# Moving every weight and work buffer of a convolution-plus-feed-forward kernel to multiples of 2 KB

## The chip, the cores and the metric

The kernel runs on one core of a Trainium2 chip. The metric is the device time of one execution in microseconds (us); lower is better. Engines are named as in the profile: PE (TensorE matmuls), PEld (TensorE weight loads), DVE (VectorE), ACT (ScalarE), POOL (GpSimd), SP (SyncE). On-chip memory has 128 partitions, and a tile occupies the same range of bytes in each of them; "at byte n" means n bytes from the start of a partition.

## What is computed

The input x is [8, 4096, 192] in float32. Eight heads of 24 channels each get their own causal filter of seven taps, whose weights are a softmax over the taps. The result, seen as 32,768 tokens of 192 channels, goes through a feed-forward layer with a rational activation:

```python
w = softmax(weight)                        # [8 heads, 7 taps]
x[b, s, head] = sum_k w[head, k] * x_padded[b, s + k, head]
h = x @ w_in                               # 192 -> 2048
P = a0 + a1*h + a2*h**2 + a3*h**3
Q = 1 + |b0|*|h| + |b1|*h**2
out = (P / (Q + 1e-6)) @ w_out             # 2048 -> 192
```

Everything is float32 and must stay near float32 accuracy.

## The kernel before, in words

The 32,768 tokens are worked in 64 chunks of 512. For each chunk, PE computes the filter as many small banded matmuls (L299) from the input tile xs (two buffers of 6,912 bytes, one for even and one for odd chunks) and the band tile wb_t. ACT and DVE bring the result to memory as a high part xh and a low part xl, 2,048 bytes each, in the reduced float32 form float32r that PE reads.

The first matrix product, here gemm1 (L334), is cut into 8 units for each chunk, each a [128, 2 x 512] tile hp: ten matmuls for a unit, five for each half, which use the weights wh_t (high part) and wl_t (low part, 16,384 bytes each) as stationary operand and xh or xl as moving operand of 512 columns. With 64 chunks that makes 512 units and 5,120 matmuls. For each unit, ACT, POOL and DVE compute the rational function: ACT copies hp to hs (L379) and makes A = |.| (L399) and B = the square (L402); POOL makes t from hs (L385, L392) and issues a DMA that adds B to A in memory (L405); ACT takes the logarithm (L408) and the exponential, y (L411); DVE does four instructions of 128 x 1024 (L396, L415, L420, L424), of which the last writes g, the activated unit.

The second product, gemm2 (L351), uses slices of g (512 bytes) as stationary operand and slices of wo_t (192 columns, 768 bytes) as moving operand, in plain float32: 4,096 matmuls in the code, each of which stands as two records in the profile. ACT copies each result to ob, and SP stores it.

The order of all this is written out by hand: the strings START, PLAN and END give the order of steps for the first chunks, for each chunk in the middle and for the last ones, and each engine follows it. The tile framework puts in the semaphores. Before the loop, the weights are loaded, rounded and split into high and low parts.

Memory: a pool is a region, and the pools lie one behind another in the order in which they are opened: const, xpool (xh, xl), work (t, A, B, four buffers each), hpool (hs, three), gpool (g, eleven), opool (ob, two), apool. Within const the tiles lie in the order of the `const.tile` calls, each rounded up to 32 bytes. Bytes 0 to 16,511 are taken by a scratch area of 16,384 bytes and four constants. These are the places of the large tiles in the kernel before:

| tile | byte | past a multiple of 2,048 | past a multiple of 256 |
|---|---|---|---|
| wb_t | 16,512 | 128 | 128 |
| xs0, xs1 | 18,400 and 25,312 | 2,016 and 736 | 224 and 224 |
| wh_t, wl_t, wo_t | 32,224, 48,608, 64,992 | 1,504 | 224 |
| one_t, neg_t, cf, sq, mx, sm | 77,280 to 78,431 | | |
| xh, xl; t, A, B; hs; g; first ob | from 78,432 | 608 | 96 |

Of the kernel before, what the change touches and what calls it, by code (L numbers as in the profile page):

```python
# [10 lines left out]
F32 = mybir.dt.float32  # L11
F32R = mybir.dt.float32r
# [12 lines left out]
P = 128  # L25
# [9 lines left out]
NG = 6  # L35
# [77 lines left out]
def kernel(  # L113
# [14 lines left out]
    const = ctx.enter_context(tc.tile_pool(name="const", bufs=1))  # L128
# [13 lines left out]
    mk_t = const.tile([P, BW], F32, name="mk_t")  # L142
    wr_t = const.tile([P, NG, KT], F32, name="wr_t")
    ab_t = const.tile([P, 6], F32, name="ab_t")
    nc.scalar.dma_start(out=wr_t, in_=wrep)
    nc.scalar.dma_start(out=ab_t, in_=ab)
    nc.scalar.dma_start(out=wb_t, in_=wband)
# [1 line left out]
    W = 2 * CH  # L149
    XF = 32 * NBLK * NG  # L150
    xs_buf = [const.tile([P, XF], F32, name=f"xs{i}") for i in range(2)]

    def clear_x(t):
        nc.gpsimd.memset(t[0:BLK, 3 * XF // 4:], 0.0)
        nc.gpsimd.memset(t[BLK:, 0:3 * XF // 4], 0.0)
# [31 lines left out]
    nc.scalar.preload_act_table_set("natural_log_exp_and_others")  # L187


    one_t = const.tile([P, P], F32, name="one_t")  # L190
    neg_t = const.tile([P, P], F32R, name="neg_t")
    nc.gpsimd.memset(one_t, 1.0)
    nc.gpsimd.affine_select(out=one_t, in_=one_t, pattern=[[1, P]], compare_op=ALU.is_equal, fill=0.0,
                            base=0, channel_multiplier=-1)
# [10 lines left out]
    load_x(1)  # L205


    cf = const.tile([P, 6], F32, name="cf")
    sq = const.tile([P, 2], F32, name="sq")
    a0, a1, a2, a3 = (cf[:, i:i + 1] for i in range(4))  # L210
    be0, be1 = cf[:, 4:5], cf[:, 5:6]
    sq1, rq = sq[:, 0:1], sq[:, 1:2]
    mx = const.tile([P, NG], F32, name="mx")
    sm = const.tile([P, NG], F32, name="sm")
    nc.vector.tensor_reduce(out=mx, in_=wr_t, axis=AX.X, op=ALU.max)
    nc.vector.tensor_tensor(out=wr_t, in0=wr_t, in1=mx[:, :, None].broadcast_to([P, NG, KT]), op=ALU.subtract)
    nc.scalar.activation(out=wr_t, in_=wr_t, func=AF.Exp)
# [313 lines left out]
```

## Time and profile before

| | |
|---|---|
| median of 3 runs | 2,733.33 us (2,733.18 to 2,734.33) |
| time of the profiled execution | 2,734.59 us |
| its span, first to last instruction | 2,732.9 us |
| mean granted clock of TensorE | 0.997 of full speed |
| busy: PE / DVE / ACT / POOL | 2,696.7 / 2,588.5 / 2,563.2 / 2,318.2 us |

The busy time of an engine is the time in which at least one of its instructions runs; matmuls overlap at their ends in the record, so the pace of PE is read from the distance between starts, not from the length of one record. A wait is named by the instruction that waited and the one that released it.

### The profile page before, as it was taken

To read this page: it belongs to the slowest core of one execution; us is meant where nothing else is said; L and a number is where in the kernel's file an instruction comes from. 1 tells how busy PE (TensorE), PEld (TensorE's weight loads), DVE (VectorE), ACT (ScalarE), POOL (GpSimd) and SP (SyncE) were. 2 spreads that over 40 slices of the span, in tenths; PEclk is the share of its full clock that TensorE was granted. 3 is DMA by queue.
4 is the path that set the end of the run, shared out by engine and by line. 5 is a ranking of instruction groups with operands and counts; after the bars stand their busy time and mean duration, and the time that the engine had idled before them with its cause. 6 is when DMAs were issued, how large, how long until landed. Compare 5 with 4: busy or idle time off the path is not lost.

```text
span 2732.9 us, 51350 instructions
## 1 busy us (share of the span) xinstructions
PE 2696.7 (99%) x20248; PEld 2418.7 (89%) x20248; DVE 2588.5 (95%) x2285; ACT 2563.2 (94%) x2927; POOL 2318.2 (85%) x1575
## 2 busy tenths in 40 slices
PE   6999999999999999999999999999999999999999
PEld 4898899898989998998998889989989998899898
DVE  7999999999999999999999999999999999999997
ACT  7999999999999999999999999999999999999996
POOL 9888888888888888888888888888888888888885
PEclk9999999999999999999999999999999999999999
DMA  7565566656665656656666656565666565666654
GB/s 188 108 124 120 120 126 120 124 117 122 123 121 118 126 119 123 123 119 124 121 121 123 120 117 128 117 126 120 119 123 125 116 125 119 120 125 121 124 104 92
DMA packets 122786, 332.79 MB, mean 122 GB/s; under 512 B 12848, under 2 KB 51888, under 8 KB 122544
## 3 DMA queue, kind: packets, MB, share of 16 engines
q0 software_dynamic: 73728, 268.47, 51.9%
q1 hardware_dynamic: 48384, 60.83, 7.9%
q8 instruction: 159, 2.61, 0.4%
q14 instruction: 83, 0.68, 0.1%
q10 hardware_dynamic: 432, 0.20, 0.0%
HBM read 35.85 MB, written 25.17 MB: 22 GB/s over the span
## 4 chain that ended last, share of the span: by engine, by line
PE 95%; ACT 2%; POOL 1%; issue 1%; DVE 1%; DMA 0%; ACTq 0%; POOLq 0%; DVEq 0%
PE op L351 48%; PE hp L334 43%; PE cps L299 4%; POOL t L392 0%; PE cps L351 0%; ACT hs L379 0%; ACT A L399 0%; ACT y L411 0%; ACT B L408 0%; DMA A<-B 0%; ACT B L402 0%; POOL t L385 0%; DMA wb_t<-in_wband 0%; DVE t L396 0%; ACT op L252 0%
## 5 line engine op out<-in xcount | busy, mean ns | idle before, releaser
L351 PE MATMUL op<-wo_t,g 128*128 128x192 f32 x8128 | 1412.3, 327 | 0.9 <-DVE wo_t L266 0.7
L351 PEld LDWEIGHTS op<-wo_t,g 128*128 128x128 f32 x8128 | 1342.7, 190 | 45.0 <-POOL t L392 1.4
L392 POOL TENSOR_TENSOR t<-t,hs 128x1024 f32<-128x1024 f32 x512 | 1267.7, 2476 | 31.8
L385 POOL TENSOR_SCALAR t<-hs,cf 128x1024 f32<-128x1024 f32 x512 | 646.8, 1263 | 299.9 <-ACT hs L379 294.5
L334 PE MATMUL hp<-xh,wh_t 128*128 128x512 f32 x2048 | 878.2, 429 | 10.1 <-DVE t L396 9.7
L415 DVE SCALAR_TENSOR_TENSOR g<-t,cf,y 128x1024 f32<-128x1024 f32 x512 | 655.2, 1280 | 91.5 <-ACT y L411 74.9
L396 DVE SCALAR_TENSOR_TENSOR t<-t,cf,hp 128x1024 f32<-128x1024 f32 x512 | 651.9, 1273 | 6.0 <-POOL t L392 4.0
L379 ACT COPY hs<-hp 128x1024 f32<-128x1024 f32 x512 | 525.3, 1026 | 133.2 <-PE hp L334 128.7
L424 DVE SCALAR_TENSOR_TENSOR g<-y,g 128x1024 f32<-128x1024 f32 x512 | 626.9, 1224 | 17.5
L334 PE MATMUL hp<-xh,wl_t 128*128 128x512 f32 x2048 | 643.3, 395 | 0.0
L420 DVE SCALAR_TENSOR_TENSOR y<-A,y 128x1024 f32<-128x1024 f32 x512 | 625.7, 1222 | 0.0
L408 ACT ACTIVATE B<-A 128x1024 f32<-128x1024 f32 x512 | 551.2, 1077 | 2.4 <-DMA A<-B 2.4
L411 ACT ACTIVATE y<-B 128x1024 f32<-128x1024 f32 x512 | 536.5, 1048 | 3.2 <-DVE g L424 2.3
L405 POOL DMA_DIRECT2D A<-B x512 | 481.1, 940 | 65.6 <-ACT A L399 42.0
L399 ACT ACTIVATE A<-hp 128x1024 f32<-128x1024 f32 x512 | 532.7, 1040 | 0.5 <-PE hp L334 0.5
L402 ACT ACTIVATE B<-hp 128x1024 f32<-128x1024 f32 x512 | 529.3, 1034 | 1.5
L334 PEld LDWEIGHTS hp<-xh,wh_t 128*128 128x128 f32 x2048 | 387.3, 189 | 89.7 <-DVE t L396 12.6
L334 PEld LDWEIGHTS hp<-xh,wl_t 128*128 128x128 f32 x2048 | 385.8, 188 | 88.7
L334 PE MATMUL hp<-xl,wh_t 128*128 128x512 f32 x1024 | 404.7, 395 | 0.0
L334 PEld LDWEIGHTS hp<-xl,wh_t 128*128 128x128 f32 x1024 | 195.9, 191 | 22.6
L299 PEld LDWEIGHTS cps<-wb_t,xs 128*32 128x32 f32 x6876 | 121.3, 150 | 53.9 <-issue 49.5
L299 PE MATMUL cps<-wb_t,xs 128*32 128x58 f32 x6876 | 137.6, 228 | 16.3 <-DVE wb_t L224 13.2
(56 smaller groups left out, 381.6 us busy)
## 6 DMA issues: line engine op xcount, KB each, us to landing
A<-B POOLq DMA_DIRECT2D x512, 512.0 KB, 4.8
out<-ob SPq DMA_DIRECT2D x128, 192.0 KB, 2.0
xs<-in_xa SPq DMA_DIRECT2D x64, 324.0 KB, 4.0
xs<-in_xb SPq DMA_DIRECT2D x64, 108.0 KB, 3.8
g<-in_w_in SPq DMA_DIRECT2D x8, 512.0 KB, 7.1
g<-in_w_out SPq DMA_DIRECT2D x8, 384.0 KB, 9.9
wb_t<-in_wband ACTq DMA_DIRECT2D x1, 174.0 KB, 5.7
wr_t<-in_wrep ACTq DMA_DIRECT2D x1, 21.0 KB, 4.4
```

The lines of the kernel that those rows point to most:

```text
L334: nc.tensor.matmul(H[k][:, j, :], lhsT=w[:, i, part, j, :], rhs=x, start=(n == 0), stop=(n == len(terms) - 1))
L351: nc.tensor.matmul(op[:, t, 0:D], lhsT=g[:, f % 2, tok:tok + P], rhs=wo_t[:, f, :], start=(f == 0 and t == 0), stop=(f == FT - 1 and t == 1))
L385: nc.gpsimd.tensor_scalar(tile_of(k, "t", work), st[k]["hs"], a3, a2, ALU.mult, ALU.add)
L392: nc.gpsimd.tensor_tensor(out=t, in0=t, in1=st[k]["hs"], op=ALU.mult)
L396: nc.vector.scalar_tensor_tensor(out=t, in0=t, scalar=a1, in1=flat(k), op0=ALU.add, op1=ALU.mult)
L399: nc.scalar.activation(out=tile_of(k, "A", work), in_=flat(k), func=AF.Abs, scale=scales[0])
L402: nc.scalar.activation(out=tile_of(k, "B", work), in_=flat(k), func=AF.Square, scale=scales[1])
L408: nc.scalar.activation(out=st[k]["B"], in_=st[k]["A"], func=AF.Ln, bias=C_Q)
L411: nc.scalar.activation(out=tile_of(k, "y", ps_y), in_=st[k]["B"], func=AF.Exp, scale=-1.0)
L415: nc.vector.scalar_tensor_tensor(out=G[k].rearrange("p a b -> p (a b)"), in0=st[k]["t"], scalar=a0, in1=st[k]["y"], op0=ALU.add, op1=ALU.mult)
L420: nc.vector.scalar_tensor_tensor(out=y, in0=st[k]["A"], scalar=C_Q, in1=y, op0=ALU.add, op1=ALU.mult)
L424: nc.vector.scalar_tensor_tensor(out=g, in0=st[k]["y"], scalar=2.0, in1=g, op0=ALU.subtract, op1=ALU.mult)
```

## The change

The six small tiles of `const` that were allocated last (one_t, neg_t, cf, sq, mx, sm; 1,152 bytes in all after rounding) are allocated ahead of the input tiles, a pad of 160 bytes follows them, and a pad of 1,280 bytes follows the two input tiles. The pads are never written or read. No other line changes.

```diff
     ab_t = const.tile([P, 6], F32, name="ab_t")
+    one_t = const.tile([P, P], F32, name="one_t")
+    neg_t = const.tile([P, P], F32R, name="neg_t")
+    cf = const.tile([P, 6], F32, name="cf")
+    sq = const.tile([P, 2], F32, name="sq")
+    mx = const.tile([P, NG], F32, name="mx")
+    sm = const.tile([P, NG], F32, name="sm")
+
+    const.tile([P, 40], F32, name="pad0")
...
     xs_buf = [const.tile([P, XF], F32, name=f"xs{i}") for i in range(2)]
+    const.tile([P, 320], F32, name="pad1")
...
-    one_t = const.tile([P, P], F32, name="one_t")
-    neg_t = const.tile([P, P], F32R, name="neg_t")
     nc.gpsimd.memset(one_t, 1.0)
...
-    cf = const.tile([P, 6], F32, name="cf")
-    sq = const.tile([P, 2], F32, name="sq")
     a0, a1, a2, a3 = (cf[:, i:i + 1] for i in range(4))
...
-    mx = const.tile([P, NG], F32, name="mx")
-    sm = const.tile([P, NG], F32, name="sm")
```

## Rows read from the trace of the kernel before

**Rows 1.** The page: busy us (share of the span) of each engine; granted clock in 40 slices.

```profile
PE 2696.7 (99%) x20248; PEld 2418.7 (89%) x20248; DVE 2588.5 (95%) x2285; ACT 2563.2 (94%) x2927; POOL 2318.2 (85%) x1575
...
PEclk9999999999999999999999999999999999999999
```

**Rows 2.** Busy time by stretches: stretch, length, engines in us, clock, DMA share, GB/s.

```profile
0.00:100.00 100.00, 68.29 (x542) 50.09 (x543) 77.92 (x95) 83.25 (x116) 91.79 (x77) 0.91 0.65 161
...
1200.00:1700.00 500.00, 500.00 (x3783) 449.90 (x3782) 479.13 (x420) 474.26 (x539) 426.35 (x288) 1.00 0.61 122
...
2600.00:2733.00 133.00, 129.15 (x832) 119.08 (x831) 114.88 (x99) 107.52 (x121) 92.96 (x63) 1.00 0.50 100
```

**Rows 3.** The page: the chain that ended last, shares of the span by line.

```profile
PE op L351 48%; PE hp L334 43%; PE cps L299 4%; POOL t L392 0%; PE cps L351 0%; ACT hs L379 0%; ACT A L399 0%; ACT y L411 0%; ACT B L408 0%; DMA A<-B 0%; ACT B L402 0%; POOL t L385 0%; DMA wb_t<-in_wband 0%; DVE t L396 0%; ACT op L252 0%
```

**Rows 4.** The chain in order of time, 1,200 to 1,242 us: start, length, what.

```profile
1204.86 2.33 PE hp L334 x10
1207.19 2.60 PE op L351 x16
...
1225.37 2.32 PE hp L334 x10
1227.69 3.25 PE op L351 x20
```

**Rows 5.** Waits, 200 to 2,600 us: total us, times, longest.

```profile
POOL t L385 <- ACT hs L379: 266.8, 365, 1.7
ACT hs L379 <- PE hp L334: 116.6, 227, 0.8
...
PE hp L334 <- DVE t L396: 0.5, 1, 0.5
```

**Rows 6.** Timeline of 1,204.5 to 1,207.1 us, PE and PEld: start, length.

```profile
1204.93 0.39 PE L334 MATMUL hp<-xl,wh_t 128*128 128x512 f32 x1
1204.94 0.19 PEld L334 LDWEIGHTS hp<-xh,wh_t 128*128 128x128 f32 x1
1205.17 0.39 PE L334 MATMUL hp<-xh,wh_t 128*128 128x512 f32 x1
...
1205.86 0.40 PE L334 MATMUL hp<-xh,wh_t 128*128 128x512 f32 x1
...
1206.10 0.40 PE L334 MATMUL hp<-xl,wh_t 128*128 128x512 f32 x1
...
1206.33 0.39 PE L334 MATMUL hp<-xh,wh_t 128*128 128x512 f32 x1
```

**Rows 7.** Single lines, 200 to 2,600 us: shortest/median/longest ns; then L408's mean.

```profile
L424 DVE SCALAR_TENSOR_TENSOR g<-y,g x459: 1224/1224/1226, 202.7 to 2596.9; 128x1024 f32<-128x1024 f32 x153
...
L415 DVE SCALAR_TENSOR_TENSOR g<-t,cf,y x460: 1271/1280/1283, 200.2 to 2599.6; 128x1024 f32<-128x1024 f32 x154
...
L408 ACT ACTIVATE B<-A x459: 1043/1064/1152, 201.9 to 2596.1; 128x1024 f32<-128x1024 f32 x153
...
L408 ACT ACTIVATE B<-A 128x1024 f32<-128x1024 f32 x512 | 551.2, 1077 | 2.4 <-DMA A<-B 2.4
```

**Rows 8.** The page: DMA issues, KB each, median us from issue to landing.

```profile
A<-B POOLq DMA_DIRECT2D x512, 512.0 KB, 4.8
```

**Rows 9.** The chain in order of time, 0 to 110 us: its longest DMA piece.

```profile
60.58 7.01 DMA A<-B
```

**Rows 10.** Busy time by stretches, 44.8 to 47.2 us; the clock is the number 0.50.

```profile
44.80:47.20 2.40, 2.40 (x7) 1.92 (x6) 2.40 (x3) 2.40 (x5) 2.40 (x3) 0.50 0.75 140
```

**Rows 11.** Timeline of PE, 43.5 to 48.5 us.

```profile
44.18 0.80 PE L334 MATMUL hp<-xh,wh_t 128*128 128x512 f32 x1 [2.07 <-DVE t L396]
44.78 0.63 PE L334 MATMUL hp<-xl,wh_t 128*128 128x512 f32 x1
45.20 0.63 PE L334 MATMUL hp<-xh,wh_t 128*128 128x512 f32 x1
45.63 1.05 PE L334 MATMUL hp<-xh,wl_t 128*128 128x512 f32 x2
```

## Prediction

> **What bounds the kernel now.** I read the busy times first. PE is busy 2,696.7 of 2,732.9 us at a granted clock of nine tenths or more in every slice [rows 1], so the reader should look for the 36 us in which it isn't. The table by stretches finds them: 31.7 us in the first 100 us, 3.9 us in the last 133, and between 100 and 2,600 us next to nothing; the stretch 1,200 to 1,700 has PE busy 500.00 of 500, with DVE at 479.13, ACT at 474.26 and POOL at 426.35 [rows 2]. The chain that ended last says the same: 48% of it are gemm2 (L351), 43% gemm1 (L334) and 4% the filter's matmuls (L299), 95% PE together [rows 3]. In order of time the chain alternates between a block of ten gemm1 matmuls in 2.33 us and blocks of gemm2 records, 16 in 2.60 us or 20 in 3.25 [rows 4]. The waits between 200 and 2,600 us are almost all those of engines that wait for PE or for one that did (POOL for ACT 266.8 us, ACT for PE 116.6); PE's own largest is 0.5 us [rows 5].
>
> So the time is a start-up, then PE's instructions one after the other, and nothing else counts unless another engine becomes slower than PE. Two pace numbers carry everything: gemm1 at 2.325 / 10 = 232.5 ns a matmul, 512 units of 10, that is 5,120 x 0.2325 = 1,190 us; gemm2 at 2.60 / 16 = 162.5 ns a record, 8,192 of them, 1,331 us [rows 4].
>
> **The change part by part.** No instruction is added, removed or reordered: the four helper groups of `const` are only allocated earlier, and the two pads are written and read by nobody. No queue, DMA, wait or semaphore moves. What changes is the byte at which each tile begins within its partition.
>
> Worked out from the tile sizes (each rounded up to 32 bytes): before, wh_t, wl_t and wo_t lie 1,504 bytes past a multiple of 2,048, and all of xpool, work, hpool, gpool and the first ob 608 past one. After, 1,312 bytes go ahead of the two xs tiles (1,152 of small constants, 160 of pad0), and 1,280 of pad1 behind them. So wh_t moves up by 2,592 bytes to byte 34,816 = 17 x 2,048; the work buffers move up by 1,440 (2,592 less the 1,152 that no longer lie ahead of them), since 608 + 1,440 = 2,048. Two things follow. Against one another all work buffers keep their distances, as they move together; only weights against work buffers change, by 1,152 bytes. And before, every large operand began 32 bytes past a multiple of 64; after, at a multiple of 64, 256 and 2,048.
>
> *PE in gemm2, 8,192 records.* Twice 192 columns at 2.4 GHz (granted clock 1.00, [rows 2]) are 160.0 ns, and 162.5 is measured. Its operands lie askew before (g slices as weights, wo_t slices as moving operand, at the offsets above), some of its slices cross a multiple of 2 KB and others don't, and the blocks of 16 and 20 give 162.5 regardless [rows 4]. The most that a better place can give is 2.5 x 8,192 = 20 us; a dearer record than 162.5 shows nowhere, so the upper end is 0 here. I take 0, since the pace is nearer to its columns than to any other price.
>
> *PE in gemm1, 5,120 matmuls.* 512 columns at 2.4 GHz are 213.3 ns, and 232.5 is measured: a surcharge of 19.2 ns. This is the one place where the layout could have a price now, and its lower end is all of it: 19.2 x 5,120 = -98 us. For the upper end, single starts within a block lie 0.22 to 0.24 us apart (1,204.93 to 1,205.17; 1,205.86 to 1,206.10) [rows 6]; if all took 0.24, +7.5 x 5,120 = +38 us. I take 0. The matmuls begun at 1,205.86 and at 1,206.10 hold the same slice of wh_t and take 0.24 and 0.23, so the spread isn't one of weight addresses; and the slices, 512 bytes apart, already stand at four different places against the moving operand.
> The Trainium skill, page "TensorE: Matmul & The Clock Gate", section "Back-to-back issue gap", gives N / 2.4 + 2.5 ns, 216 ns for 512 columns, as the gap of an isolated warm matmul. The trace agrees in gemm2 (162.5 for 384 column times) and disagrees in gemm1 by 16.7 ns; by the page the sum would be 5,120 x 16.7 = 86 us lower if the place in memory were what stands between, by the row it is unchanged.
>
> *DVE, ACT and POOL* run under PE. Cheaper instructions there give nothing. The price if the cover goes: DVE has 20.9 us of slack in 500, 4.2%. Its 128 x 1024 instructions keep their time whatever of the 11 g buffers they write (L424: 1,224 to 1,226), and the dearest of this shape is 1,283 (L415) [rows 7]; were all 4.8% dearer, as 1,283 to 1,224, DVE would stand at 502 of 500, level with PE. ACT has 5.1% of slack. Its L408 costs 1,077 in the mean and 1,152 at most [rows 7]; were all ACT work 7% dearer, ACT would need 507.5 for each 500, +37 us over the 2,500 us. I take 0 for both, as by the row L424 is blind to which buffer it is given.
>
> *DMA.* The 512 accumulating DMAs (A <- B) land in 4.8 us [rows 8], and all of ACT's waits for them come to 2.4 us (L408, [rows 7]). In the start-up one of them stands in the chain with 7.01 us [rows 9]; wb_t, the first thing waited for there, doesn't move. Between 0 and all of the 2.4 us can be won; a DMA as long as the worst here, 7.01 for 4.8, still has no waiter in the steady part. I take -0.2 us.
> The page "DMA: Bandwidth & Descriptors" of the Trainium skill, section "How a descriptor splits into AXI transactions", says that one beginning off a multiple of 256 bytes reads from the boundary below. A 4,096-byte row that starts 96 bytes past one would so be 17 transactions instead of 16, and 131 beats instead of 128, an estimate of 2.3% of a DMA's time; no run here shows it yet. By it A <- B would land some 0.1 us sooner, and the sum stays as it is.
>
> *Sum:* gemm2 0, gemm1 0, engines under cover 0, DMA -0.2. The profiled execution has 2,734.59 us, 1.69 around its span; the median of the three runs, 2,733.33, is 1.26 below it. From that median: 2,733.1 us.
>
> **The rivals.** *The surcharge of gemm1 goes (faster).* If the 19.2 ns are what reading from skew addresses costs, and 2.5 stay as in gemm2, 5,120 x 16.7 = 86 us go: 2,648; at half of it 2,690. For it: in the few matmuls at half clock (0.50 between 44.8 and 47.2 us, the 1.2 GHz level, [rows 10]), after PE had waited 2.07 us, starts lie 0.42 to 0.43 us apart, and 512 / 1.2 is 427 ns [rows 11]. There the surcharge is gone, so it isn't a fixed number of column times; something with its own speed, such as the supply of operands, lies behind it. Against it: gemm2, just as askew, doesn't pay; but it takes 768 bytes of moving operand in 162.5 ns, half the rate of gemm1's 2,048 in 232.5, so this isn't proof. And the weight load offers another cause: each begins when the matmul before starts, and the next matmul comes 0.23 to 0.24 us after it [rows 6], whatever the place. Chance 0.20.
>
> *Weights and moving operand get in step (slower).* Before, they start 896 bytes apart within 2 KB; after, both at 0. If PE's two reads then meet in the same part of the memory, each gemm1 matmul waits longer. Place: L334; price: at 0.24 each, 2,771. It decides from 1.1 ns a matmul on (5.5 us / 5,120). For it: nothing hides PE, and starts do vary between 0.22 and 0.24. Against: the four slices of a weight already vary that distance by 512-byte steps, and blocks keep to 2.32 to 2.33 us. Chance 0.15.
>
> *The change does not take effect.* The pads could be dropped, or the addresses be others than I worked out. Then nothing moves at all: 2,733.3. Chance 0.02, which joins the forecast's 0.63.
>
> **How the numbers follow.** 0.2% (5.5 us) is about what a measurement here can tell from no change. Forecast with the idle change: 0.65 within 2,728 to 2,739. The faster rival 0.20, the slower 0.15. The forecast's own range leaves out 0.35; reaching half way into the smaller sizes of each rival (3.4 ns a matmul less, 17 us, and 2.5 more, 13 us) leaves some 0.18 outside: 2,716 to 2,746. A full-sized rival, 2,648 or 2,771, lies outside on purpose.
>
> **What would show it.** Right: blocks of ten gemm1 matmuls at 2.32 to 2.33 and of 16 gemm2 records at 2.60, PE busy 500 of 500, DVE and ACT within 1% of 479 and 474. The faster rival shows as blocks of ten nearing 2.16, and ACT's wait for PE shrinking first; the slower one as blocks of 2.40. My prediction is wrong if gemm1's pace depends on the address at all, or if ACT or DVE instructions grow by more than 4%: then their busy time passes PE's.

## The result and the profile after

After: 2,720.15 us, median of 5 runs (2,718.13 to 2,721.96); before, in the same comparison, 2,733.18 (2,732.50 to 2,734.33). The ratio is 0.9950 with a 95% interval of 0.9937 to 0.9963: 13 us or 0.5% faster. That lies inside the range of 2,716 to 2,746 and outside the 0.2% that the forecast called likeliest; it fell to the side that had 0.20. Times are medians of the runs at the undisturbed clock; one run with everything 32 further, at a granted clock of 0.753 (3,395 us), and one of before, at 0.85 (3,030 us), are left out.

The line numbers of the kernel after are higher by 3 in the loops: gemm1 is L337, gemm2 L354, the filter's matmuls L302. The page and the table by stretches, as in [rows 1] and [rows 2]:

```profile
PE 2682.7 (99%) x20248; PEld 2414.5 (89%) x20248; DVE 2584.0 (95%) x2285; ACT 2561.4 (94%) x2927; POOL 2313.8 (85%) x1575
...
PEclk9999999999999999999999999999999999999999
```

```profile
0.00:100.00 100.00, 66.93 (x544) 48.46 (x544) 77.36 (x95) 83.44 (x116) 92.31 (x78) 0.93 0.64 161
...
1200.00:1700.00 500.00, 500.00 (x3796) 451.74 (x3795) 480.74 (x422) 476.38 (x541) 427.77 (x289) 1.00 0.59 122
```

PE has lost 14.0 us of busy time (2,696.7 to 2,682.7) and the span 12.6 (2,732.9 to 2,720.3); the other engines kept theirs to within 4.5. In 500 us all engines now do a little more of the same work, and PE is still busy for all of it. So the same instructions run, PE sets the time as before, and its instructions got shorter. Which ones the chain in order of time shows, beside [rows 4]:

```profile
1209.38 2.30 PE hp L337 x10
1211.68 2.60 PE op L354 x16
1214.28 2.28 PE hp L337 x10
1216.56 3.25 PE op L354 x20
1219.81 2.32 PE hp L337 x10
```

gemm2 keeps 16 records in 2.60 us and 20 in 3.25. The blocks of ten gemm1 matmuls, 2.32 to 2.33 before, now take 2.28, 2.30 or 2.32: 2.28 behind 16 gemm2 records, 2.32 as before behind 20. Starts within a block show it too, against the 0.23 and 0.24 of [rows 6]:

```profile
1205.33 0.39 PE L337 MATMUL hp<-xh,wh_t 128*128 128x512 f32 x1
1205.55 0.39 PE L337 MATMUL hp<-xl,wh_t 128*128 128x512 f32 x1
1205.78 0.39 PE L337 MATMUL hp<-xh,wh_t 128*128 128x512 f32 x1
```

The waits between 200 and 2,600 us are those of [rows 5], a little shorter, as the others now have less time to wait for PE:

```profile
POOL t L388 <- ACT hs L382: 256.5, 339, 1.7
ACT hs L382 <- PE hp L337: 97.9, 169, 0.8
```

and the DVE and ACT instructions of [rows 7] cost what they did (shortest/median/longest ns):

```profile
L427 DVE SCALAR_TENSOR_TENSOR g<-y,g x461: 1223/1224/1226, 201.8 to 2595.0; 128x1024 f32<-128x1024 f32 x154
...
L411 ACT ACTIVATE B<-A x462: 1044/1067/1156, 201.1 to 2598.7; 128x1024 f32<-128x1024 f32 x154
```

Two measures are used from here on, both taken from the starts of gemm1 matmuls in the trace. The *unit time* is the distance from the first matmul of unit 50 (counted from 0) to that of unit 482, divided by 432. Before, these start at 289.00 and 2,547.90 us, which gives 5.229 us; after, at 287.73 and 2,536.24:

```profile
287.73 0.53 PE L337 MATMUL hp<-xh,wh_t 128*128 128x512 f32 x1
...
2536.24 0.53 PE L337 MATMUL hp<-xh,wh_t 128*128 128x512 f32 x1
```

That is 5.205 us, 24 ns less for each unit, and 512 x 24 = 12.3 of the 12.6 us. The *eight gaps* are the time from the start of the second matmul of a block to that of the tenth, as a mean: 1,858.5 ns before (232.3 each), 1,841.1 after (230.1 each).

The mean after is one of unlike blocks. Between 200 and 2,600 us the blocks behind 16 gemm2 records went from 1,858.4 to 1,823.9 ns, those behind 20 only from 1,858.3 to 1,855.4 (171 to 174 blocks in each of the four means, worked out from the starts in the traces). The order of steps is fixed, so the first are always units 1, 2 and 4 of a chunk and the others 0, 5 and 6; no run tells whether the unit or what runs ahead of it makes the difference. A value of the eight gaps below is such a mean.

### The profile page after: what moved, and what is told of

The parts are those of the page before. It is cut to its first block, busy times and chain, and to the rows that moved or that the text cites. A ratio compares the mean times of both kernels' runs of the same rounds, so it can differ in the third digit from the quotient of the medians.

```text
span 2720.3 us, 51350 instructions
## 1 busy us (share of the span) xinstructions
PE 2682.7 (99%) x20248; PEld 2414.5 (89%) x20248; DVE 2584.0 (95%) x2285; ACT 2561.4 (94%) x2927; POOL 2313.8 (85%) x1575
## 4 chain that ended last, share of the span: by engine, by line
PE 96%; ACT 2%; POOL 1%; issue 1%; DVE 0%; DMA 0%; ACTq 0%; POOLq 0%; DVEq 0%
PE op L354 48%; PE hp L337 43%; PE cps L302 5%; POOL t L395 0%; PE cps L354 0%; ACT B L411 0%; ACT hs L382 0%; ACT A L402 0%; ACT B L405 0%; DMA wb_t<-in_wband 0%; ACT y L414 0%; POOL t L388 0%; DVE t L399 0%; PE cps L279 0%; ACT op L255 0%
## 5 line engine op out<-in xcount | busy, mean ns | idle before, releaser
L354 PE MATMUL op<-wo_t,g 128*128 128x192 f32 x8128 | 1410.6, 327 | 1.5 <-DVE wo_t L269 1.3
L354 PEld LDWEIGHTS op<-wo_t,g 128*128 128x128 f32 x8128 | 1341.5, 190 | 43.0 <-POOL t L395 2.0
L337 PE MATMUL hp<-xh,wh_t 128*128 128x512 f32 x2048 | 871.2, 425 | 8.9 <-DVE t L399 8.5
L337 PE MATMUL hp<-xh,wl_t 128*128 128x512 f32 x2048 | 636.9, 392 | 0.0
L408 POOL DMA_DIRECT2D A<-B x512 | 480.2, 938 | 66.4 <-ACT A L402 52.9
L337 PEld LDWEIGHTS hp<-xh,wl_t 128*128 128x128 f32 x2048 | 385.5, 188 | 89.5
L337 PEld LDWEIGHTS hp<-xh,wh_t 128*128 128x128 f32 x2048 | 386.2, 189 | 83.0 <-DVE t L399 12.2
L337 PE MATMUL hp<-xl,wh_t 128*128 128x512 f32 x1024 | 404.4, 395 | 0.0
L337 PEld LDWEIGHTS hp<-xl,wh_t 128*128 128x128 f32 x1024 | 193.8, 189 | 20.2
L302 PEld LDWEIGHTS cps<-wb_t,xs 128*32 128x32 f32 x6876 | 121.4, 150 | 53.9 <-issue 49.3
L302 PE MATMUL cps<-wb_t,xs 128*32 128x58 f32 x6876 | 137.7, 228 | 17.2 <-DVE wb_t L227 14.3
```

What stands on the lines that cost most here:

```text
L337: nc.tensor.matmul(H[k][:, j, :], lhsT=w[:, i, part, j, :], rhs=x, start=(n == 0), stop=(n == len(terms) - 1))
L354: nc.tensor.matmul(op[:, t, 0:D], lhsT=g[:, f % 2, tok:tok + P], rhs=wo_t[:, f, :], start=(f == 0 and t == 0), stop=(f == FT - 1 and t == 1))
```

## The experiments

Places are given as bytes past a multiple of 2,048 for the weights (W: wh_t, wl_t, and wo_t unless said otherwise), for gemm1's moving operand (X: xh, xl) and for the other buffers (t, A, B, hs, g). "X - W" is the distance from weights to moving operand within 256 bytes; why 256 the sweeps show. The two runs without the other engines and the two sweeps were taken once each, and only their pace counts.

| kernel | W | X | others | X - W | time, us | ratio to before (95%) | unit time, us | eight gaps, ns |
|---|---|---|---|---|---|---|---|---|
| before | 1,504 | 608 | 608 | 128 | 2,733.18 | | 5.229 | 1,858.5 |
| after | 0 | 0 | 0 | 0 | 2,720.15 | 0.9950 (0.9937 to 0.9963) | 5.205 | 1,841.1 |
| weights at 0, buffers at 608 | 0 | 608 | 608 | 96 | 2,738.06 | 1.0017 (1.0007 to 1.0026) | 5.239 | 1,869.7 |
| weights at 1,504, buffers at 0 | 1,504 | 0 | 0 | 32 | 2,736.62 | 1.0011 (1.0001 to 1.0021) | 5.235 | 1,867.0 |
| everything 32 further | 32 | 32 | 32 | 0 | 2,720.43 | 0.9951 (0.9935 to 0.9967) | 5.208 | 1,840.9 |
| both at 1,024 | 1,024 | 1,024 | 1,024 | 0 | 2,719.36 | 0.9953 (0.9936 to 0.9969) | 5.200 | 1,837.8 |
| X with weights, others off | 0 | 0 | 608 | 0 | 2,721.33 | 0.9954 (0.9938 to 0.9971) | 5.205 | 1,841.1 |
| X alone off | 0 | 608 | 0 | 96 | 2,738.51 | 1.0016 (1.0006 to 1.0025) | 5.237 | 1,866.3 |
| after, without other engines | 0 | 0 | 0 | 0 | | | 5.202 | 1,841.3 |
| before, without other engines | 1,504 | 608 | 608 | 128 | | | 5.226 | 1,858.5 |
| X 60 past the weights, weights moved | 196 | 0 | 0 | 60 | 2,736.71 | 1.0011 (1.0001 to 1.0020) | 5.235 | 1,865.7 |
| X begins at 60 | 0 | 60 | 0 | 60 | 2,710.96 | 0.9918 (0.9904 to 0.9932) | 5.185 | 1,820.7 |

(In the last two rows W, X and the others are counted past a multiple of 256; wo_t is at 0 in both.)

**One place at a time, against the kernel after.**

```diff
     wo_t = const.tile([P, FT, D], F32, name="wo_t")
+    const.tile([P, 152], F32, name="pad2")
```

> After, with a pad of 608 bytes behind the weights: weights stay at multiples of 2 KB, the work buffers (moving operand of gemm1, A, B, g) go back to 608 past one. Theory 'place of the weights' (what counts is where wh_t, wl_t, wo_t begin): about 2,720 us, as after. Theory 'place of the moving operand' and theory 'shorter DMAs' (A and B at multiples of 256): about 2,733, as before. Theory 'distance' (weights against buffers, 896 before, 0 after, here 608 the other way round): another value than after, not forecast which.

```diff
-    const.tile([P, 320], F32, name="pad1")
+    const.tile([P, 184], F32, name="pad1")
...
+    const.tile([P, 136], F32, name="pad2")
```

> After, with the last 544 bytes of pad1 moved behind the weights: weights back at 1,504 past a multiple of 2 KB, work buffers stay at multiples of 2 KB. 'Place of the weights': about 2,733. 'Place of the moving operand' and 'shorter DMAs': about 2,720. 'Distance': 544, another value than after, not forecast which.

Measured 2,738.06 and 2,736.62: neither the weights at 2 KB nor the buffers at 2 KB keep anything of the gain; either alone is even dearer than before.

```diff
-    const.tile([P, 40], F32, name="pad0")
+    const.tile([P, 48], F32, name="pad0")
```

> After, with pad0 32 bytes longer, so that input tiles, weights and buffers all begin 32 past a multiple of 64; all distances as after. 'Distance': 2,720. Any theory by which a start at a multiple of 64 or more counts (weights, moving operand or DMAs): about 2,733.

```diff
-    const.tile([P, 320], F32, name="pad1")
+    const.tile([P, 576], F32, name="pad1")
```

> After, with pad1 1,024 bytes longer: weights and buffers 1,024 past a multiple of 2 KB, distances between them as after, all starts at multiples of 1 KB. 'Distance', 'shorter DMAs' and any theory with a line of up to 1 KB: 2,720. A theory by which the multiple of 2 KB itself counts (a moving operand of 2,048 bytes in one 2 KB block instead of two): about 2,733.

Measured 2,720.43 and 2,719.36: both keep the whole gain. With everything 32 past a multiple of 64, not one operand is better aligned than before. So a start at a multiple of 64, 256 or 2,048 is not what helps; the distances are. The first of these two also settles the DMAs. There the accumulating DMAs land as late as before:

```profile
q0 software_dynamic: 73728, 268.47, 51.9%
...
A<-B POOLq DMA_DIRECT2D x512, 512.0 KB, 4.8
```

and in the kernel after they are quicker, with 50.0% of the queues' time:

```profile
q0 software_dynamic: 73728, 268.47, 50.0%
...
A<-B POOLq DMA_DIRECT2D x512, 512.0 KB, 4.6
```

The times differ by 0.3 us. The shorter DMAs are real and bring nothing that can be measured.

**Which distance: PE's two reads, or PE against the other engines?** In the first kernel a pad pool stands between xpool and work; in the second, pads stand ahead of and behind xpool.

```diff
     xpool = ctx.enter_context(tc.tile_pool(name="xpool", bufs=2))
+    px = ctx.enter_context(tc.tile_pool(name="px", bufs=1))
+    px.tile([P, 152], F32, name="px")
     work = ctx.enter_context(tc.tile_pool(name="work", bufs=4))
```

> Weights and xpool (xh, xl: the moving operand of gemm1) at multiples of 2 KB as after; a pad of 608 bytes ahead of the work pool, so that t, A, B, hs and g lie 608 past one. If the distance that counts is that of PE's own two reads (weights against xh, xl): about 2,720. If it is that of PE's reads against the buffers which DVE, ACT, POOL and the DMAs use: 2,733 to 2,738.

```diff
+    px.tile([P, 360], F32, name="px")
...
     wo_t = const.tile([P, FT, D], F32, name="wo_t")
+    const.tile([P, 152], F32, name="pad2")
```

> The reverse: weights and t, A, B, hs, g at multiples of 2 KB, xh and xl alone 608 past one. PE's own two reads: about 2,738, as with weights at 0 and all buffers at 608. The other engines' buffers: about 2,720.

Measured 2,721.33 and 2,738.51, as the theory of PE's own two reads has it, to 2 us. The first also puts gemm2's operands apart (g at 608, wo_t at 0) and loses nothing by it.

**PE by itself.** The element-wise steps of chunks 3 to 59 are left out, once in the kernel after and once in the kernel before:

```diff
+            elif 3 <= c < NCH - 4:
+                if kind == "m":
+                    G[c * UPC + n] = G[c * UPC + n - UPC]
+                elif kind == "g":
+                    del H[c * UPC + n]
             else:
                 unit_steps[kind](c * UPC + n)
```

> The layout of after, with the element-wise steps of chunks 3 to 59 left out (gemm1, the filter and gemm2 stay; gemm2 reads the activations of an earlier chunk), so that ACT, DVE, POOL and the DMAs are nearly idle there. Only the pace of gemm1 in that stretch is read. If PE's two reads get in each other's way by themselves, gemm1 keeps some 230 ns a matmul here and some 232 in the layout of before. If other engines cause the surcharge, both layouts come near 216 (512 columns at 2.4 GHz and the 2.5 ns of gemm2).

> The same work left out, in the layout of before. PE's own two reads: a block of ten gemm1 matmuls 20 to 24 ns longer than in the layout of after. Other engines: as long as there, near 2.16 us.

The busy times of 600 to 800 us (PE, PEld, DVE, ACT, POOL), first in the layout of after:

```profile
600.00:800.00 200.00, 200.00 (x1538) 180.63 (x1537) 7.68 (x15) 10.93 (x24) 0.00 (x0) 1.00 0.08 22
```

then in the layout of before:

```profile
600.00:800.00 200.00, 200.00 (x1534) 179.97 (x1533) 7.68 (x15) 11.41 (x25) 0.00 (x0) 1.00 0.08 22
```

POOL has nothing to do, DVE and ACT are busy for 4% and 6%, the DMA share has fallen from 0.6 to 0.08, and PE is where it was: eight gaps of 1,841.3 and 1,858.5, the same to 0.2 ns as with all engines at work. This is shown, then: the surcharge of gemm1 is there with the other engines nearly idle, and the part of it that the change removed hangs on the place of PE's moving operand against its weights. That all of the surcharge arises there is not shown. The unlike blocks of the kernel after are there too: 1,823.3 behind 16 gemm2 records and 1,855.8 behind 20.

**Sweeping the distance.** In the kernel without the other engines' work, all gemm1 matmuls of a chunk read their moving operand from one copied tile at an offset of that chunk's own, with weights at 0:

```diff
+        if 3 <= c < NCH - 4:
+            if k == 3 * UPC and j == 0:
+                for q in range(2):
+                    nc.scalar.copy(out=xsw[:, q * CH:(q + 1) * CH], in_=xhA.bitcast(F32))
+            o = OFF[c - 3] // 4
+            xhA = xlA = xB = xsw[:, o:o + CH]
```

> As the run without other engines, layout of after, but in chunks 3 to 59 all gemm1 matmuls read their moving operand from one copied tile, which begins at a multiple of 2 KB, at an offset that differs from chunk to chunk: multiples of 64 bytes from 0 to 1,984, then some between, then 0, 1,152, 608 and 544 once more. Only the pace of gemm1 by chunk is read. If the distance between PE's two reads sets the surcharge, offset 0 gives some 2.30 us for ten, 1,152 (the distance of before) 2.32, 608 and 544 2.33. If the distance has a period of 64 bytes, all multiples of 64 are alike and others dearer; if single places within 2 KB matter, the multiples of 64 differ among themselves. If the tile's own place or the buffers' neighbours mattered instead, the offsets would all give one value.

The eight gaps in ns, a mean over the eight units of each chunk, grouped by the offset within 256 bytes:

```
offset                                     eight gaps
  0 + 256 n, n = 0 to 7 (0 twice)          1837.5 to 1842.1
 64 + 256 n, n = 0 to 7                    1841.2 to 1843.6
128 + 256 n, n = 0 to 7 (1,152 twice)      1858.6 to 1860.2
192 + 256 n, n = 0 to 7                    1862.9 to 1867.2
 32 + 256 n: 32, 288, 544, 800, 1056       1865.8 to 1866.9
 96 + 256 n: 96, 352, 608, 864, 1120       1865.8 to 1868.6
160 + 256 n: 160, 416, 928                 1869.2 to 1872.1
224 + 256 n: 224, 480, 736, 992            1860.4 to 1862.2
4, 8, 16, 48, 80, 112                      1891.2, 1870.0, 1850.4, 1863.4, 1847.5, 1842.2
```

Places 256 bytes apart are alike, and within 256 bytes they differ by some 50 ns. The sweep agrees with the whole kernels in the table above: 128 gives 1,859 (before: 1,858.5), 96 gives 1,866 to 1,869 (1,869.7 and 1,866.3), 32 gives 1,866 to 1,867 (1,867.0), 0 gives 1,842 (1,841). The theory of a period of 64 falls, as 64 and 128 differ by 17 ns.

The same kernel with other offsets:

> The sweep again, with offsets in steps of 8 bytes from 0 to 248, nine in steps of 4, and sixteen of them once more 512 or 1,024 bytes further. Theory 'period of 256 bytes': the repeats equal their first, to within 3 ns on eight gaps. In the coarse sweep the eight gaps of a block came to about 1,842 ns at 0 and 64 (and 112), 1,847 at 80, 1,860 at 128, 1,867 at 192 and 32. If the best distance is one of these, nothing in the fine sweep lies below 1,840; a value well below would be a better layout than after.

```
offset      0     8    12    16    20    24    32    40    48    56    60    64    68    72    76
eight   1839.5 1871.8 1834.0 1850.5 1889.6 1873.1 1867.4 1870.0 1864.9 1844.9 1821.5 1842.1 1891.5 1878.1 1827.9
offset     80    84    88    96   104   108   112   116   120   124   128   144   176   208   240   248
eight   1846.8 1879.9 1867.9 1868.6 1865.9 1851.5 1841.9 1895.1 1878.0 1839.0 1859.0 1860.5 1858.8 1862.5 1886.8 1851.5
```

The expectation that nothing lies below 1,840 was wrong. Offset 60 costs 1,821.5, and four of the five offsets that are 12 past a multiple of 16 (12, 60, 76, 124) are among the best, while the four that are 4 past one (20, 68, 84, 116) are among the dearest, 1,880 to 1,895. Ten offsets between 136 and 232 that are not shown lie between 1,859.8 and 1,876.9. Of the sixteen repeats, twelve came within 3 ns of their first; those of 112, 120, 176 and 208 missed by 3.2 to 8.1 (the worst: 1,862.5 and 1,870.6 at 208), so the period holds in the large and not to the nanosecond.

**The best distance in the whole kernel.** First by moving the weights, in tiles 64 words longer, with SKEW = 49 words:

```diff
+    SKEW = 49
...
-    wh_t = const.tile([P, UPC, 2, 2, P], F32R, name="wh_t")
-    wl_t = const.tile([P, UPC, 2, 2, P], F32R, name="wl_t")
+    wh_t = const.tile([P, UPC * 4 * P + 64], F32R, name="wh_t")[:, SKEW:SKEW + UPC * 4 * P]
+    wh_t = wh_t.rearrange("p (i a b c) -> p i a b c", i=UPC, a=2, b=2)
+    wl_t = const.tile([P, UPC * 4 * P + 64], F32R, name="wl_t")[:, SKEW:SKEW + UPC * 4 * P]
+    wl_t = wl_t.rearrange("p (i a b c) -> p i a b c", i=UPC, a=2, b=2)
```

> The whole kernel in the layout of after, but wh_t and wl_t begin 196 bytes past a multiple of 256, so that the moving operand lies 60 bytes past the weights, counted within 256: the best place of the fine sweep (1,821.5 ns on eight gaps against 1,839.5 to 1,842 at 0). If the distance between PE's two reads is all that counts, down to the word, and the sweep holds for the whole kernel: 18 to 20 ns on eight gaps, some 23 on ten, times 512, 12 us below after: about 2,708. If what counted in the sweep was that the moving operand itself began off a multiple of 16 (here the weights do): 2,720 or above.

Measured 2,736.71, eight gaps 1,865.7: the same distance of 60, and none of the gain. The theory that the distance alone counts, down to the word, falls. Then by moving the operand itself:

```diff
+    SKEW = 15
...
-        xh = xpool.tile([P, CH], F32R, name=f"xh{half}")
+        xh = xpool.tile([P, CH + 64], F32R, name=f"xh{half}")[:, SKEW:SKEW + CH]
...
-            xl = xpool.tile([P, CH], F32R, name="xl")
+            xl = xpool.tile([P, CH + 64], F32R, name="xl")[:, SKEW:SKEW + CH]
```

> The whole kernel in the layout of after, but xh and xl begin 60 bytes past a multiple of 256 (in tiles 256 bytes longer), weights at multiples of 2 KB, as in the fine sweep at offset 60. The run with the weights 196 past showed that the distance alone doesn't settle it below a step of 16 bytes. If the place of the moving operand within its 16 bytes is the other condition: 18 to 20 ns on eight gaps less than after, about 2,708, unless the filter's ACT and DVE instructions, which now write at odd words, grow by more than their slack. If the sweep's value came from its single shared moving tile: 2,720 or above.

Measured 2,710.96 (2,710.71 to 2,712.47), ratio 0.9918, interval 0.9904 to 0.9932: 22 us under before and 9 under after, the fastest kernel of this study. The eight gaps fell by 20.4 ns, as the sweep had said, and the unit time by 20 ns, which is 10 of the 12 us expected. All blocks are alike here, 1,821.7 ns behind 16 gemm2 records and 1,821.6 behind 20: against after, nearly all of the gain lies in the blocks that had kept the pace of before or part of it. Its blocks in the chain:

```profile
1208.60 2.28 PE hp L338 x10
1210.88 3.25 PE op L355 x20
```

Between 1,200 and 1,242 us every full block without the filter ahead of it takes 2.27 or 2.28 us. DVE and ACT do not pay for the odd words in their instructions on xh and xl: the DVE subtraction that writes xl takes 684 ns in the mean, as in the kernel before, whose line stands first.

```profile
L317 DVE TENSOR_TENSOR xl<-cps,xh 128x512 fp32r<-128x512 f32 x64 | 43.8, 684 | 4.4 <-ACT xh L308 4.4
...
L321 DVE TENSOR_TENSOR xl<-cps,xh 128x512 fp32r<-128x512 f32 x64 | 43.8, 684 | 3.2 <-ACT xh L312 3.2
```

## Why the prediction was right in its range and wrong in its likeliest case

*What bounds the kernel:* right. PE sets the time before and after; the runs without the other engines' work show it best, with unit times of 5.202 and 5.226 us against 5.205 and 5.229.

*gemm2 at 0:* right, 16 records in 2.60 us in every layout shown.

*Engines under cover at 0:* right. DVE and ACT keep their busy time, and PE's gain passes to the end undiminished, as they have slack.

*DMA at -0.2:* right in effect. The estimate of 2.3% that the prediction worked out from the Trainium skill's page "DMA: Bandwidth & Descriptors", section "How a descriptor splits into AXI transactions", has the right sign: landing went from 4.8 to 4.6 us and the share from 51.9% to 50.0%, about 4%. The kernel with everything 32 further shows both back at 4.8 us and 51.9%, and its time at 2,720.

*gemm1 at 0:* this is the step that failed. The term was mis-sized: -12.3 us instead of 0, within its bounds of -98 and +38. By a sign that the prediction gave itself, "wrong if gemm1's pace depends on the address at all", its account of gemm1 was wrong. That the time still lies in the range is no merit of that account: the range had been opened by 17 us for a small size of the faster rival. The reason that was given for the 0 was that the weight slices, 512 bytes apart, "already stand at four different places against the moving operand". The sweeps show that 512 is twice the period, so the four slices stood at one and the same place, 128 within 256. The even pace of 2.32 to 2.33 was read as a proof of indifference, and it only said that the layout had never varied. The same holds for the eleven g buffers. The other reason compared two matmuls that hold the same slice of wh_t; the slice that loads beside each is the next one, and all of them stood alike within 256.

*The filter's matmuls* have no term in the sum, though they hold 4% of the chain. The prediction said that only weights against work buffers change; in fact the input tiles xs, the filter's stationary operand, moved by 1,312 bytes against wb_t, its moving operand. Nothing came of it, 137.6 us busy before and 137.7 after:

```profile
L299 PE MATMUL cps<-wb_t,xs 128*32 128x58 f32 x6876 | 137.6, 228 | 16.3 <-DVE wb_t L224 13.2
...
L302 PE MATMUL cps<-wb_t,xs 128*32 128x58 f32 x6876 | 137.7, 228 | 17.2 <-DVE wb_t L227 14.3
```

*The faster rival* had the place right (L334) and the cause wrong. It made skew addresses the cause; with everything 32 further they are as skew as before, and the gain stays. Its count for gemm2, "half the rate" of gemm1, takes each record for one read of 768 bytes, while the sum takes a record for twice 192 columns; were the bytes read twice as well, the rate would be 1,536 bytes in 162.5 ns, above gemm1's. *The slower rival* was right that PE's two reads matter to one another and had the wrong sign for this change: both at 0 is quicker. Other distances do cost time, +0.1 to +0.2% with the weights alone or the moving operand alone at 0; that the two reads meet in the same part of the memory is not shown.

The page "TensorE: Matmul & The Clock Gate" of the Trainium skill says in section "Step-by-step: what each phase is for" that PE has two independent read ports and that loading the next weights takes no read bandwidth from the running matmul. The runs without other engines show that the two reads still do not leave one another alone: the eight gaps are 1,841.3 or 1,858.5 ns, by the place of the moving operand against the weights. Whether it is read bandwidth that is lost is not shown.

*What stays open.* At the best place found, eight gaps are 1,820.7 ns, 227.6 each, against 213.3 for the columns; whether the remaining 14 ns are also a matter of place is not known. Why 60 helps when the moving operand is moved and not when the weights are is open too: in the second case the weights begin at 4 past a multiple of 16 and the moving operand at 0, and no run separates these. Open, too, is why the blocks behind 20 gemm2 records gain 3 ns at a distance of 0 and those behind 16 some 34, and why the moving operand at 60 makes them alike. With X at the weights and the other buffers off, the mean is that of after, but the two kinds stand at 1,836.1 and 1,851.5. That the memory is interleaved with a period of 256 bytes would fit the sweeps; it is argued, not shown.

## What to carry to other kernels

Where PE is busy without a gap and its matmuls take longer than their columns, the place of the weights against the moving operand is worth a sweep: it costs no instruction, and one kernel that changes the offset from chunk to chunk measures dozens of places in one run. An even pace over many slices proves nothing if all slices are the same distance apart in the period that counts; look at the strides before calling a term insensitive. Round addresses are no aim in themselves: with everything 32 bytes further the gain stayed, and the best version found begins its moving operand at byte 60. Below 16 bytes the distance alone does not foretell the pace, so measure each layout in the whole kernel. And look at single blocks before trusting a mean: here one number stood for blocks that gained some 34 ns and blocks that gained 3.

## What the hardware showed that was not expected

- With float32r operands of 512 columns, each with its own weight load, the pace depends on the place of the moving operand against the weights, with a period of 256 bytes to within 8.1 ns: 1,821 to 1,895 ns for eight gaps, 4% between best and dearest.
- It does so to the word: offsets 60 and 68, 8 bytes apart, give 1,821.5 and 1,891.5.
- At one and the same distance, 0, blocks can differ by their place in the order of work: 1,823.9 ns behind 16 gemm2 records, 1,855.4 behind 20.
- Other engines have no part in it: with POOL at 0 and DVE at 4% the eight gaps are the same to 0.2 ns.
- gemm2, float32 with 192 columns, kept 162.4 ns a record with its operands 128 apart within 256 (before), 0 (after) and 96 (g at 608, wo_t at 0).
